# One fewer second-level token pair in two weight groups of a spectral mixer, with the work around the group change re-timed

## The chip, the cores and the metric

The kernel runs on one core of a Trainium2 chip. The metric is the device time of one execution in microseconds; the time of a kernel is the median of several executions. The engines named below are TensorE (PE, with its weight loads as PEld), VectorE (DVE), ScalarE (ACT), GpSimd (POOL) and SyncE (SP). SP and POOL issue the transfers.

## The reference

The kernel computes, for two batches of 4096 tokens of width 640, a gated mix of two branches:

```python
x = A_x
g = _sigmoid((x * gate_w).sum(-1, keepdims=True))
a = _A_ref(x, A_w1, A_b1, A_w2, A_b2)     # FFT over tokens, block-diagonal complex MLP, soft shrinkage, inverse FFT
b = _B_ref(x, B_w_gate, B_w_up, B_w_down) # (gelu(x @ w_gate) * (x @ w_up)) @ w_down, hidden width 1728
return g * a + (1 - g) * b
```

All arithmetic keeps about float32 precision. The kernel gets that from the matmul type fp32r by splitting each operand into a high and a low part and summing three products (high·high, high·low, low·high).

## The kernel before, in words

The first third of the span, and the place of the change, is the product `x @ [w_gate, w_up]` of branch B. The 8192 tokens are cut into 16 *token pairs* of 512 columns (two halves of 256). The hidden width is cut into 14 *weight tiles* of 128 columns, each with a gate and an up matrix, and the tiles are handled in three *groups*: tiles 0 to 3, 4 to 7 and 8 to 13. `keys` lists the (group, token pair) steps: steps 0 to 15 are group 0, steps 16 to 31 group 1 (token pairs in the order 1, 2, 0, 3, ... 15), steps 32 to 47 group 2. Each step calls `quad` once per weight tile (`plain` in step 0).

`quad` computes gate and up for both halves of a token pair with a Strassen-like scheme: seven block products in place of eight, on sums and differences ("forms") of token blocks (`b11`, `k4`, `t3`, `b21`, `t2`, `t5`, `t1`, `b22`, `t4`) and of weight blocks (`g1`, `g2`, `s1` to `s4`, `u2`). A call is 54 matmuls of 128x256. Part of its work (`half5`, `half3`, `half4`) is put off into the next call.

There is a second level. For the product of `g2` with `b21`, two token pairs (an odd one and the following even one) and two weight tiles form another 2x2 block, which `deep_parts` does with seven products instead of eight, 21 matmuls instead of 24. `deep(key)` says where: groups 0 and 1, token pairs 3 to 14. A deep `quad` leaves out its own six matmuls on `b21` and keeps partial results (`PB`, `h`) until the seven products have been added in (L695); these products are slipped into the next three calls by `extra`. Token forms for the second level are made by `x_deep` in group 0 (sums, then five split parts), stored to `xA` in memory, and loaded again in group 1; weight forms are made by `w_deep`.

The order of work is written out by hand. Each `quad` has seven hooks, so a step of groups 0 and 1 has 28 *slots*. `spread(i, s, fs)` puts functions into slots of step `i` from slot `s` on, running over into the next step; `at(i, j, f)` runs one after call `j` of step `i`. Each engine takes its instructions in the order in which they are written. What is placed so:

- `x_prep(nxt, k)` makes form `k` of the next step's token pair: a source (a VectorE subtraction or a raw tile), a high part on ScalarE, a low part on VectorE. In group 0 the forms `t1` to `t4` are also stored to `xD` through POOL's queue, and in most of group 1 they are loaded from there on SP's queue.
- `x_raw` loads the raw token tiles of the step after next, at the end of a step.
- `w_raw(t)` loads the two raw matrices of a weight tile of the next group; `w_prep(t)` makes its forms in eight stages.
- The forward Fourier transform of branch A is spread over steps 17 to 45 as 64 *elements* (`a_seq`), each a load `a_load`, two splits `a_split`, a gate sum `a_gate` and two halves of products `a_step`. `steps_a` says in which step an element sits, `A_POINTS` in which slots. Its tables come in four loads `f1_load`, the first three of which belong to elements 0, 18 and 38 and the last to 58.

On-chip buffers are pools of equal slots: 18 "big" (weights, `PB`, Fourier tables), 14 "mid" (token forms), 18 "small" (raw tiles, sums, `h`, Fourier data), 15 "tiny". A new tile waits until the last user of its slot is done. Stores are collected by `st` and issued on SP's queue at the end of the next call.

After these 48 steps follow the spectral MLP (L983 to L1124), and the down projection fused with the inverse transform (L1406, L297); the change does not touch their code.

Of the kernel before, what the change touches and what calls it, by code (L numbers as in the profile page):

```python
# [10 lines left out]
F32 = mybir.dt.float32  # L11
# [4 lines left out]
P = 128  # L16
# [7 lines left out]
CW = CH + 2  # L24
NCH = 8
NPAIR = 13
FIRST = 3

# [184 lines left out]
def spectral_mix_kernel(ctx: ExitStack, tc: tile.TileContext, a):  # L215
# [9 lines left out]
    dram = ctx.enter_context(tc.tile_pool(name="dram", bufs=1, space=bass.MemoryType.DRAM))  # L225
# [29 lines left out]
    def flush():  # L255
        for dst, src in late:
            ld(dst, src)
        late.clear()
# [5 lines left out]
    hD = dram.tile([64, P, 14 * P], F32, name="hD")  # L264
    wdf = [dram.tile([P, 13 * 320], F32, name=f"wdf_{j}") for j in range(7)]
    wdl = dram.tile([P, 7 * 320], F32, name="wdl")
    xA = {t: dram.tile([P, 3584], F32, name=f"xA_{t}") for t in range(FIRST, 15, 2)}

    fny = consts.tile([P, 8], F32, name="fny")
    sgn = consts.tile([P, 4], F32, name="sgn")  # L270
# [36 lines left out]
    GR, WA, XA, PEND = {}, {}, {}, {}  # L307

    def deep(key):
        return key[0] < 2 and FIRST <= key[1] < 15  # L310

    def w_raw(t):
        RAW[t] = []
# [132 lines left out]
    def x_raw(key, names=("b11", "b21", "b12", "b22", "k4")):  # L446
        d = XT.setdefault(key, {})
        for n in names:
            if (key[0] != 1 or made(key) or n != "b12") and not (key[0] == 1 and deep(key) and n == "b21"):
                r = d[n] = small([P, 512], name="xraw")  # L450
                ld(r, a["xT"][key[1], ("b11", "b21", "b12", "b22", "k4").index(n)])
# [6 lines left out]
    def x_prep(key, k, eng=nc.vector):  # L458
# [35 lines left out]
        def lo():  # L494
# [4 lines left out]
            if kept is not None:  # L499
                nc.gpsimd.dma_start(xD[key[1]][:, kept],  # L500
                                    XM.pop((key, name)).rearrange("p h n -> p (h n)").bitcast(F32))
        return [lambda: None] * 3 if name == "b21" and deep(key) else [src, hi, lo]

    def x_deep(gr, tp):
# [77 lines left out]
    def quad(key, t, hook):  # L582
# [7 lines left out]
        old = Q.pop() if Q else [lambda: None] * 3  # L590

        dp = deep(key)
        ahead_ = dp and key[1] % 2 == 1
        X = half()
# [167 lines left out]
    def mixed(key):  # L762

        o, w = XO[key], WG[NPAIR]
        ws = [(w[:, k, 0], w[:, k, 1]) for k in range(5)]
        pm = bank()
        for q, (x0, x1) in enumerate((("b11", "b21"), ("b12", "b22"))):
            run(pm[:, 256 * q:256 * q + 256], prod(ws, x_of(o, x0, x1, ("k4", q))))
        s, h = small([P, 512], name="gelu"), small([P, 512], name="h")
        nc.gpsimd.memset(h[64:], 0.0)  # L770
        nc.scalar.activation(s[:64], pm[:64], AF.Gelu_apprx_tanh)
        nc.scalar.activation(h[:64], pm[64:], AF.Copy)
        nc.vector.tensor_mul(h[:64], s[:64], h[:64])
        h_store(key[1], NPAIR, h)
# [713 lines left out]
    def at(i, j, f, *args):  # L1488
        todo.setdefault((i, j), []).append((f, *args))
# [57 lines left out]
    def spread(i, s, fs):  # L1547

        for k, f in enumerate(fs):
            j, q = i, max(s + k, 0)  # L1550
            while j < last and q >= points(j):
                j, q = j + 1, q - points(j)
            slots.setdefault((j, q), []).append(f)
    steps_a = [(i, j) for i in (*range(17, 30), *range(32, 46)) for j in ((0, 1) if i < 32 else (0, 1, 2) if 32 < i < 43 else (0, 2))]

    def back(i, s, f):
        if s < 0:
# [2 lines left out]
    for k, (b, n2) in enumerate(a_seq):  # L1560
        i, j = steps_a[k]
# [16 lines left out]
    for i, (gr, tp) in enumerate(keys):  # L1578
        if deep((gr, tp)) and tp % 2:
            p, f = x_deep(gr, tp)  # L1580
# [9 lines left out]
    for k, (l, pb) in enumerate(((1, 0), (1, 1), (2, 0), (2, 1))):  # L1590
        s0 = (5, 12, 19, 26)[k]
        f = prep(l, pb)
# [2 lines left out]
        spread(last, s0 + 1, f[2:])  # L1595
    for gr in range(2):
        for k, t in enumerate(groups[gr + 1]):
            (i, j), (i2, s) = [((14, 1), (15, 0)), ((14, 3), (15, 8)), ((15, 0), (15, 17)), ((15, 2), (16, 4)), ((15, 3), (16, 12)), ((15, 1), (15, 25))][k]
            at(16 * gr + i, j, w_raw, t)
            spread(16 * gr + i2, s, w_prep(t))  # L1600
    for j in range(7):
# [6 lines left out]
    for i, key in enumerate(keys):  # L1608
        gr, tp = key
        nxt = keys[i + 1] if i < last else None  # L1610
        quads = [t for t in groups[gr] if t < NPAIR]
        nq = len(quads)
        if nxt:
            if not i:
                x_raw(nxt)
            z = 7 * (nq - 1)
            for k, s in enumerate((5, 8, 11, 14, 16, 18, z + 1, z + 4, z + 6) if gr < 2 else
                                  (6, 9, 13, 17, 21, z + 1, z + 2, z + 3, z + 3, z + 5)):
                if k < 9 or nxt[0] == 2:
                    f0, f1, f2_ = x_prep(nxt, k)  # L1620
                    spread(i, s - 1, [f0])
                    spread(i, s + 1, [f1, f2_])
            if gr < 2 and nxt[0] == 2:
                spread(i, z + 7, x_prep(nxt, 9))
        for j, t in enumerate(quads):
            def hook(k):
                for f in slots.get((i, 7 * j + k), ()):
                    f()
            (quad if i else plain)(key, t, hook)
            if gr == 2 and j == 1:  # L1630
                mixed(key)
            if i % 16 == 15:
                WG.pop(t)
            if 0 < i + 1 < last and j == nq - 1:
                x_raw(keys[i + 2])
            n = len(late)
            for f, *args in todo.get((i, j), []):
                f(*args)
            new = late[n:]
            del late[n:]  # L1640
            flush()
            late.extend(new)
        for q in range(7 * nq, 7 * nq + 14) if i == last else ():
            for f in slots.get((i, q), ()):
                f()
        XO.pop(key)
# [131 lines left out]
```

## Time and profile before

| what | value |
|---|---|
| median of three runs | 2539.72 us (2539.08 to 2541.27) |
| the profiled execution | 2539.19 us, its span 2537.4 us |
| TensorE clock granted | 1.00 throughout |
| matmuls on PE | 20227, busy 2526.0 us |
| VectorE / ScalarE / POOL busy | 2085.4 / 1491.6 / 388.7 us |
| DMA | 502.65 MB, mean 198 GB/s |

Step 15, the last of group 0, lies at about 370 to 400 us from the start of the span; step 31, the last of group 1, at about 781 to 811 us.

In the profile, L562 is a product inside `quad`, L694 one of the second level, L817 one of the Fourier transform. L278 and L281 are the helpers that write the high and the low part of a split, so their lines are told apart by the tile: `xo` token forms, `xs` either a second-level token form or Fourier data, `w` weight forms, with `wt` their sums and `wraw` the raw weights. L588 and L589 copy or apply gelu to a result; L616, L640, L650, L651, L655 and L659 are VectorE's additions and multiplications on results. A row of the timeline ends in the idle time before the instruction and what ended it.

### The profile page before, as it was taken

The page shows a single profiled execution, that of the slowest core. Times are in us where ns is not written, and L with a number is a line of the kernel's source. Part 1 is how long each engine was busy: PE and PEld are TensorE (multiplying, and loading weights), DVE is VectorE, ACT ScalarE, POOL GpSimd, SP SyncE. Part 2 cuts the span into 40 slices and gives each one's busy share as a digit, 9 for nine tenths or more (in the row PEclk, how much of TensorE's full clock was granted, in tenths as well). Part 3 has the DMA queues.
Part 4 walks back from the last instruction along what each step waited for, and adds up shares of the span by engine and source line. Part 5 has one row for each costly group of instructions (what it writes and reads, how often), then busy time and mean ns, then how long its engine had stood idle before and what let it go on. Part 6 is the DMA issues. An engine that isn't in the chain of part 4 may idle for free.

```text
span 2537.4 us, 54692 instructions
## 1 busy us (share of the span) xinstructions
PE 2526.0 (100%) x20227; PEld 2517.4 (99%) x20227; DVE 2085.4 (82%) x4340; ACT 1491.6 (59%) x3504; POOL 388.7 (15%) x409
## 2 busy tenths in 40 slices
PE   9999999999999999999999999999999999999999
PEld 9999999999999999999999999999999999999999
DVE  7677778777777877787667788888999999999998
ACT  5455556656555666666556788777654444444443
POOL 0111110000000000000003111111133333333332
PEclk9999999999999999999999999999999999999999
DMA  6566667777777677777767454548744444344433
GB/s 217 206 209 232 229 226 217 241 236 240 232 253 249 208 236 247 242 236 226 230 220 228 123 167 139 167 144 267 275 152 151 156 155 142 132 151 156 155 126 104
DMA packets 352511, 502.65 MB, mean 198 GB/s; under 512 B 26284, under 2 KB 223532, under 8 KB 352244
## 3 DMA queue, kind: packets, MB, share of 16 engines
q1 hardware_dynamic: 334244, 446.33, 54.5%
q0 software_dynamic: 18000, 52.83, 5.7%
q8 instruction: 159, 2.61, 0.4%
q14 instruction: 108, 0.88, 0.1%
HBM read 308.41 MB, written 190.65 MB: 197 GB/s over the span
## 4 chain that ended last, share of the span: by engine, by line
PE 93%; DVE 3%; DMA 2%; ACT 1%; issue 1%; SPq 0%; DVEq 0%; ACTq 0%
PE bank L562 49%; PE bank L1406 22%; PE bank L297 14%; PE bank L983 3%; PE bank L694 2%; PE bank L817 1%; PE bank L1064 1%; PE bank L1065 1%; DVE w L281 1%; DMA xraw<-in_xT_dram 0%; DMA s<-scr 0%; DMA xo<-xD 0%; DVE xo L281 0%; DMA hD<-h 0%; PE bank L1066 0%
## 5 line engine op out<-in xcount | busy, mean ns | idle before, releaser
L562 PE MATMUL bank<-xo,w 128*128 128x256 f32 x11100 | 1316.5, 277 | 3.7 <-ACT u L588 1.6
L562 PEld LDWEIGHTS bank<-xo,w 128*128 128x128 f32 x11100 | 1291.6, 188 | 6.6 <-ACT u L588 2.8
L1406 PE MATMUL bank<-wx,ho 128*128 128x320 f32 x3844 | 560.7, 306 | 0.0
L1406 PEld LDWEIGHTS bank<-wx,ho 128*128 128x128 f32 x3844 | 557.1, 188 | 0.0
L281 DVE TENSOR_TENSOR ho<-hraw,ho 128x640 fp32r<-128x640 f32 (+3 forms) x384 | 266.4, 735 | 20.9 <-ACT ho L278 17.9
L278 ACT ACTIVATE ho<-hraw 128x640 fp32r<-128x640 f32 x320 | 167.0, 571 | 93.6 <-PE bank L1406 70.4
L588 ACT ACTIVATE u<-bank 128x256 f32<-128x256 f32 x312 | 119.7, 384 | 154.1 <-PE bank L562 144.3
L281 DVE TENSOR_TENSOR xs<-xr,xs 64x640 fp32r<-64x640 f32 x128 | 104.9, 820 | 73.1 <-ACT xs L278 71.1
L640 DVE TENSOR_TENSOR u<-bank,u 128x256 f32<-128x256 f32 x204 | 85.8, 421 | 85.6 <-ACT u L588 83.7
L281 DVE TENSOR_TENSOR xo<-xraw,xo 128x512 fp32r<-128x512 f32 x191 | 131.2, 687 | 22.3 <-ACT xo L278 21.0
L297 PE MATMUL bank<-wm,h 128*128 128x320 f32 (+1 forms) x792 | 137.9, 309 | 0.0
L819 DVE TENSOR_TENSOR as<-bank,as 64x320 f32<-64x320 f32 x256 | 113.7, 482 | 23.5 <-ACT as L818 21.7
L278 ACT ACTIVATE xo<-xraw 128x512 fp32r<-128x512 f32 x191 | 119.6, 626 | 14.8 <-DMA xraw<-in_xT_dram 10.5
L297 PEld LDWEIGHTS bank<-wm,h 128*128 128x128 f32 (+1 forms) x792 | 117.9, 185 | 1.5 <-DVE h L1042 0.3
L562 PE MATMUL bank<-wx,ho 128*128 128x320 f32 x764 | 116.7, 307 | 0.8 <-DVE ho L281 0.8
L562 PEld LDWEIGHTS bank<-wx,ho 128*128 128x128 f32 x764 | 112.1, 188 | 1.3 <-DVE ho L281 1.1
L818 ACT ACTIVATE as<-bank 64x320 f32<-64x320 f32 x256 | 96.8, 427 | 24.1 <-PE bank L817 20.4
L588 ACT ACTIVATE p<-bank 128x256 f32<-128x256 f32 x132 | 50.7, 384 | 95.6 <-DVE h L651 53.2
L278 ACT ACTIVATE xs<-xr 64x640 fp32r<-64x640 f32 x128 | 94.0, 735 | 21.3 <-DMA xr<-in_x_dram 19.2
L278 ACT ACTIVATE ho<-hs 128x640 fp32r<-128x640 f32 (+1 forms) x128 | 68.5, 569 | 63.6 <-DVE ho L281 44.9
L770 POOL MEMSET h<- 64x512 f32 x16 | 8.4, 522 | 615.9 <-PE bank L817 314.0
L1373 ACT ACTIVATE uu<-bank,gs 128x320 f32<-128x320 f32 x120 | 54.8, 526 | 75.1 <-PE bank L297 74.5
(196 smaller groups left out, 4008.0 us busy)
## 6 DMA issues: line engine op xcount, KB each, us to landing
xo<-xD SPq DMA_DIRECT2D x124, 512.0 KB
xraw<-in_xT_dram SPq DMA_DIRECT2D x213, 256.0 KB
hD<-h SPq DMA_DIRECT2D x176, 256.0 KB
hraw<-hD SPq DMA_DIRECT2D x128, 320.0 KB
xD<-xo POOLq DMA_DIRECT2D x64, 512.0 KB, 3.6
sc<-scr SPq DMA_DIRECT2D x65, 320.0 KB
xr<-in_x_dram SPq DMA_DIRECT2D x64, 320.0 KB
scr<-as SPq DMA_DIRECT2D x64, 320.0 KB
```

The costliest lines, as they stand in the source:

```text
L278: nc.scalar.activation(dst, src, AF.Copy, scale=scale)
L281: eng.tensor_sub(dst, src, hi.bitcast(F32))
L297: nc.tensor.matmul(dst, l, r, start=i == 0, stop=i == len(ops) - 1)
L562: nc.tensor.matmul(dst, l, r, start=first and i == 0, stop=i == len(ops) - 1, skip_group_check=True)
L588: copy = lambda d, s_: nc.scalar.activation(d, s_, AF.Copy)
L640: nc.vector.tensor_add(u4, C, u4)
L694: nc.tensor.matmul(acc, l, r, start=first and i == 0, stop=i == 2, skip_group_check=True)
L818: nc.scalar.activation(stg[hi, cs], pa[lo, :320], AF.Copy)
L819: nc.vector.tensor_add(stg[hi, cs], pa[hi, :320], stg[hi, cs])
L983: nc.tensor.matmul(pz[:, kp * P:(kp + 1) * P], SC[b, c, kp][:, o:o + P], ft, start=True, stop=True)
L1373: nc.scalar.activation(uu[n2][:, cs], pe[:, :320], AF.Copy, scale=gs[:, b, 0, n2:n2 + 1])
L1406: nc.tensor.matmul((X, Y)[k], *op, start=n[k] == 0 and not (more and k), stop=n[k] == tot[k] - 1, skip_group_check=True)
```

## The change

- `deep` now ends before token pair 13: pairs 13 and 14 of groups 0 and 1 do the product of `g2` and `b21` inside `quad`. So `x_deep` and the `xA` buffer exist for pairs starting at 3, 5, 7, 9 and 11 only, and `b21` is loaded and split for pairs 13 and 14 in group 1 too.
- The first weight tile of the next group (tile 4 in group 0, tile 8 in group 1) has its raw load at the end of step 13 (29) instead of after call 1 of step 14 (30), and its preparation in slots 10 to 17 of step 14 (30) instead of slots 0 to 7 of step 15 (31).
- The first Fourier element is placed in step 14; all others move up by one place, and step 42 has two places instead of three. The loads of the tables move with them.
- Where the step is deep and the next one is not (pair 12 to 13), the forms with number above 5 (`t1`, `b22`, `t4`) of the next pair come three slots later.

```diff
-FIRST = 3
+FIRST, LAST = 3, 13
...
-    xA = {t: dram.tile([P, 3584], F32, name=f"xA_{t}") for t in range(FIRST, 15, 2)}
+    xA = {t: dram.tile([P, 3584], F32, name=f"xA_{t}") for t in range(FIRST, LAST, 2)}
...
     def deep(key):
-        return key[0] < 2 and FIRST <= key[1] < 15
+        return key[0] < 2 and FIRST <= key[1] < LAST
...
-    steps_a = [(i, j) for i in (*range(17, 30), *range(32, 46)) for j in ((0, 1) if i < 32 else (0, 1, 2) if 32 < i < 43 else (0, 2))]
+    steps_a = [(i, j) for i in (14, *range(17, 30), *range(32, 46)) for j in ((0,) if i < 16 else (0, 1) if i < 32 else (0, 1, 2) if 32 < i < 42 else (0, 2))]
...
         for k, t in enumerate(groups[gr + 1]):
-            (i, j), (i2, s) = [((14, 1), (15, 0)), ((14, 3), (15, 8)), ((15, 0), (15, 17)), ((15, 2), (16, 4)), ((15, 3), (16, 12)), ((15, 1), (15, 25))][k]
+            (i, j), (i2, s) = [((13, 3), (14, 10)), ((14, 3), (15, 8)), ((15, 0), (15, 17)), ((15, 2), (16, 4)), ((15, 3), (16, 12)), ((15, 1), (15, 25))][k]
...
             for k, s in enumerate((5, 8, 11, 14, 16, 18, z + 1, z + 4, z + 6) if gr < 2 else
                                   (6, 9, 13, 17, 21, z + 1, z + 2, z + 3, z + 3, z + 5)):
+                if k > 5 and deep(key) and not deep(nxt):
+                    s += 3
```

## The prediction

> **What bounds the kernel now.** I read the page first: busy times, then the chain.
>
> ```profile
> span 2537.4 us, 54692 instructions
> PE 2526.0 (100%) x20227; PEld 2517.4 (99%) x20227; DVE 2085.4 (82%) x4340; ACT 1491.6 (59%) x3504; POOL 388.7 (15%) x409
> PE 93%; DVE 3%; DMA 2%; ACT 1%; issue 1%; SPq 0%; DVEq 0%; ACTq 0%
> ```
>
> TensorE sets the time nearly everywhere; the chain leaves it for 7%. So every matmul added is paid, and all that can be won lies in the places where TensorE was held up. To find them I asked for equal stretches and looked for low matmul counts. The columns are stretch, its length, busy time (instructions) of PE, PEld, DVE, ACT, POOL, then clock, DMA share, GB/s. First a stretch at full pace, then the five poor ones, with a good counterpart (703.20) to one of them (651.20).
>
> ```profile
> 300.00:325.00 25.00, 25.00 (x223) 25.00 (x223) 18.79 (x43) 12.78 (x33) 4.82 (x9) 1.00 0.74 261
> 344.00:370.00 26.00, 25.69 (x226) 25.49 (x225) 19.16 (x42) 14.39 (x36) 5.35 (x10) 1.00 0.74 263
> 370.00:400.40 30.40, 28.80 (x236) 27.50 (x235) 27.24 (x78) 18.25 (x54) 1.06 (x2) 1.00 0.73 218
> 651.20:674.30 23.10, 23.01 (x193) 22.31 (x193) 15.33 (x34) 12.78 (x30) 0.00 (x0) 1.00 0.87 317
> 703.20:725.05 21.85, 21.85 (x194) 21.85 (x193) 15.72 (x35) 13.10 (x30) 0.00 (x0) 1.00 0.83 300
> 753.80:769.40 15.60, 14.56 (x128) 14.36 (x127) 5.91 (x13) 6.08 (x15) 0.00 (x0) 1.00 0.96 326
> 781.50:811.40 29.90, 28.82 (x238) 27.44 (x237) 26.74 (x77) 17.84 (x54) 0.00 (x0) 1.00 0.80 255
> ```
>
> The pace of a matmul comes from PE's timeline: 152 of them from 339.83 to the next group at 357.06, 17.23/152 = 0.1134 us each.
>
> ```profile
> 339.83 17.39 PE L562 MATMUL bank<-xo,w 128*128 128x256 f32 x152
> 357.06 0.50 PE L694 MATMUL bank<-xo,w 128*128 128x256 f32 x3
> ```
>
> A plain call of `quad` is 54 matmuls, a call under the second level 48, and each 2x2 block has seven products of three. Step 15 (370.0 to 400.4, the last token pair of group 0) is 4x54 + 21 = 237 matmuls, 26.9 us; it took 30.4, so **3.5 us are lost**. Step 31 (781.5 to 811.4) is the same work: **3.0 us**. The stretch at 753.80 holds about 126 (14.3 us) in 15.6: **1.3**. The one at 651.20 does the work of the one at 703.20 in 1.25 us more. Step 14 adds 0.5 (five matmuls short).
>
> Now the causes. In step 15 VectorE first stands and then never stops (its timeline, PE's beside it, then three quads of the step in the columns above):
>
> ```profile
> 375.34 0.50 PE L694 MATMUL bank<-xs,w 128*128 128x256 f32 x3
> ...
> 372.37 0.42 DVE L346 TENSOR_TENSOR wt<-wraw 128x256 f32<-128x256 f32 x1
> 375.88 0.43 DVE L347 TENSOR_TENSOR wt<-wt,wraw 128x256 f32<-128x256 f32 x1 [3.09 <-PE bank L694]
> ...
> 378.70:386.60 7.90, 7.84 (x65) 7.47 (x65) 7.87 (x25) 5.22 (x16) 0.27 (x1) 1.00 0.87 251
> 386.60:393.80 7.20, 6.63 (x55) 6.32 (x54) 7.20 (x21) 4.83 (x15) 0.00 (x0) 1.00 0.53 137
> 393.80:400.40 6.60, 6.43 (x55) 6.22 (x55) 6.57 (x20) 4.46 (x16) 0.53 (x1) 1.00 0.86 268
> ...
> 787.45 0.43 DVE L347 TENSOR_TENSOR wt<-wt,wraw 128x256 f32<-128x256 f32 x1 [3.09 <-PE bank L694]
> ```
>
> L347 writes a new "small" buffer for the first weights of the next group. It waits 3.09 us for L694, a product of the second level that reads `xs`, a small buffer too: all 18 are taken. After it VectorE owes three preparations, and is at 7.87 of 7.90, 7.20 of 7.20, 6.57 of 6.60. Step 31 repeats this to the hundredth.
>
> **The change, part by part.** *Plain products for pairs 13 and 14, groups 0 and 1.* Eight `quad` calls per group gain 6 matmuls each and lose two blocks of 21: +6 per group, +12 in all, 12 x 0.1134 = **+1.4 us**, with no cover.
>
> On VectorE this takes the block additions (L695, 14 per group) and the low parts of `x_deep` out of steps 14 and 15, and gives each quad one addition (L616). The prices, from the list of groups by form, then one weight preparation's `wt` instructions, and a plain step with two Fourier elements:
>
> ```profile
> L819 DVE TENSOR_TENSOR as<-bank,as 64x320 f32<-64x320 f32 x256 | 113.7, 482 | 23.5 <-ACT as L818 21.7
> L281 DVE TENSOR_TENSOR xs<-xr,xs 64x640 fp32r<-64x640 f32 x128 | 104.9, 820 | 73.1 <-ACT xs L278 71.1
> L804 DVE SCALAR_TENSOR_TENSOR xr<-xr,gw 128x640 f32<-128x640 f32 x64 | 52.2, 816 | 0.3
> L281 DVE TENSOR_TENSOR xo<-xraw,xo 128x512 fp32r<-128x512 f32 x191 | 131.2, 687 | 22.3 <-ACT xo L278 21.0
> L695 DVE TENSOR_TENSOR pb<-bank,pb 128x256 f32<-128x256 f32 x120 | 50.3, 419 | 1.3 <-PE bank L694 1.1
> L616 DVE TENSOR_TENSOR p<-bank,p 128x256 f32<-128x256 f32 x108 | 46.7, 433 | 9.6 <-PE bank L562 7.2
> ...
> 384.80:393.30 8.50, 4.01 (x12) 1.00 0.52 146
> ...
> 448.50:473.00 24.50, 24.50 (x209) 24.50 (x208) 19.07 (x42) 14.74 (x35) 1.06 (x2) 1.00 0.72 225
> ```
>
> *First weights half a pair sooner.* `w_prep` of weight tile 4 (and 8) moves from slots 0-7 of step 15 (31) to slots 10-17 of step 14 (30). It costs VectorE 4.01 for `wt` and, as estimates from the 0.82 and 0.42 rows, 1.24 for the two low parts taken from `wraw`: 5.2 us, a little high because neighbours overlap. Step 15's VectorE then has 27.24 - 5.2 - 8 block additions x 0.42 = 18.7 us of work in 4x54x0.1134 = 24.5 us, and the 3.09 us wait has no `xs` left to wait for. In group 1, `b21` of 13 and 14 is now split in steps 28 and 29 (0.69 each), where the rows from 651.20 to 753.80 show VectorE a third idle: 0. What is late next in step 15 is the pair of preparations at slots 8-25, about as long as the 2.4 quads they share; I leave 0.3 us. Step 15: -3.5 + 0.3 = **-3.2**; step 31: -3.0 + 0.3 = **-2.7**. Bounds: all of it (-6.5) and nothing. I stay near the whole since both causes are removed, not shortened.
>
> *What step 14 now carries.* The first Fourier element moves from step 17 into step 14: two splits, one gate, four additions, 2x0.82 + 0.82 + 4x0.48 = 4.4 us. Its VectorE load: 19.16 + 5.2 + 4.4 + 4x0.43 - six block additions (2.5) - five `x_deep` low parts (two of 512 columns at 0.69, three of 256 at 0.42, 2.6) = 25.4 by durations, some 23 with the overlap of neighbours, in 25.1 us of TensorE work. The plain step at 448.50 with two elements loses nothing at 19.07. So it is tight: bounds 0 and 2.3 (the load by durations plus 2 us of idle as in that stretch), taken **+0.5**, nearer the row that lost nothing. Step 30 has no element and a light load: 0. The other elements each move up one place, and step 42 has one fewer: the same work, 0.
>
> *The forms made later.* In step 14 the copy for `t2` waits for the 15th "mid" buffer (there are 14) until the next quad's first product has read `b11`:
>
> ```profile
> 362.84 1.18 PE L562 MATMUL bank<-xo,w 128*128 128x256 f32 x9
> 364.67 2.33 PE L562 MATMUL bank<-xo,w 128*128 128x256 f32 x18 [0.31 <-ACT h L588]
> ...
> 363.71 0.63 ACT L278 ACTIVATE xo<-xd 128x512 fp32r<-128x512 f32 x1 [4.20 <-PE bank L562]
> ```
>
> That is the step from a deep pair to a plain one, worth the 0.5 us lost in step 14. It moves to step 12, and only `t1`, `b22`, `t4` come three slots later, which `t2` does not profit from: 0, bounds ±0.5. In group 1 the same wait stands on SP's queue (a load of `t2`), now in step 28, where stores of `hD`, `scr` and the next loads of `xr` and `xraw` queue behind it for some 4 us; they have a quad of lead: **+0.2**, bounds 0 and 1.3 (the loss at 753.80).
>
> *Transfers.* For pair 13 the five loads of `xA` go (2x512 + 3x256 = 1792 KB) and two of `b21` come (512 KB); as many stores leave POOL's queue.
>
> ```profile
> f<-in_f_dram POOLq DMA_DIRECT2D x3, 640.0 KB, 7.0
> xo<-xA SPq DMA_DIRECT2D x12, 512.0 KB
> xs<-xA SPq DMA_DIRECT2D x18, 256.0 KB
> ...
> 754.78 0.38 SPq L524 DMA_DIRECT2D xs<-xA  x1
> 757.72 2.25 SPq L451 DMA_DIRECT2D xraw<-in_xT_dram  x4
> 764.75 0.63 ACT L278 ACTIVATE xo<-xraw 128x512 fp32r<-128x512 f32 x1 [3.35 <-DMA hD<-h]
> 765.71 3.68 PE L562 MATMUL bank<-xo,w 128*128 128x256 f32 x30 [1.04 <-ACT p L588]
> ...
> 649.06 0.54 POOL L782 DMA_DIRECT2D f<-in_f_dram  x1 [191.43 <-DMA xr<-in_x_dram]
> 661.81 0.63 ACT L278 ACTIVATE xo<-xraw 128x512 fp32r<-128x512 f32 x1 [2.42 <-DMA xraw<-in_xT_dram]
> ```
>
> At 757.72 four `xraw` are issued behind the `xA` loads with the queues 96% busy; the first is used 7 us later, and TensorE stands 1.04. Without those 1.3 MB net the first tile should land in time: -1.3 + 0.1 = **-1.2**. The second Fourier table (`f`, 640 KB) was issued at 649.06 just ahead of the `xA` and `xraw` loads, and the wait at 661.81 follows; its good twin at 703.20 has no table load. It is now asked for 17 slots (15 us) earlier, at the start of step 25, and goes out once a "big" buffer is free: between 0 and -1.25, taken **-0.8**. The first table moves to step 13, where a big buffer is free: 0. The earlier raw weights (two of 320 KB) go where the `xA` traffic was: 0.
>
> Here the Trainium skill speaks against me. DMA: Bandwidth & Descriptors, section Anatomy of one DMA, fits a load from POOL as 2.0 us plus its bytes at 436 GB/s, an estimate of 3.5 us for this table, half of the measured 7.0. By that the table is no burden, the -0.8 falls away, and the sum would be 2534.7.
>
> **The sum**: 1.4 - 3.2 - 2.7 + 0.5 + 0.2 - 1.2 - 0.8 = -5.8 us. This execution took 2539.19 (span 2537.4 and 1.8 around it), which gives 2533.4; the median of the runs is 2539.72, 0.5 above, so I say **2533.9**.
>
> **Rivals.** *There is less to win.* PE's busy columns show idle of 1.60, 1.08, 1.04 and 0.09 in steps 15, 31, at 753.80 and at 651.20, 3.8 in all, where my counts say 9.05. If only that returns: 1.4 - 3.8 + 0.7 = -1.7, 2538.0. Against it: 237 matmuls at the pace seen elsewhere fit no other length. The Trainium skill, Perfetto Trace Analysis, section Identifying the Most-Contended Engine, calls matmul busy time a poor measure and load-weights busy time a good one; PEld idles 2.90, 2.46, 1.24 and 0.79, and by it the sum is 1.4 - 7.4 + 0.7 = -5.3, 2534.4, near mine.
>
> *VectorE only moves its jam.* Step 14 fills up by the 2.3 of its upper bound and step 15's pair of preparations keeps half of each loss: 1.4 - 3.25 + 2.3 + 0.2 - 2.0 = -1.4, 2538.3.
>
> *The change doesn't do what it says*: the small buffers are short at slot 10 too, and the 3 us wait comes along with both jams: 1.4 + 0.7 - 2.0 = +0.1, 2539.8. Against it: the three `xs`, and the `h` buffers that deep quads hold for three quads, are gone by then.
>
> *Slower.* The weights wait for big buffers. Of 18, twelve hold the old weights; the Fourier table now occupies one from step 13 on and the early preparation takes three more from slot 10. Should the preparations of steps 15 and 31 find none, ScalarE stands at each until a quad has released its weights, up to 5 us; the 4.20 us wait at 363.71 cost TensorE only 0.5, so some 2.4 us are covered and 2.6 lost. It decides from three preparations per group on: 6 x 2.6 = 15.6 in place of the 6.5 lost now, +15.6 - 6.5 + 1.4 - 2.0 + 0.7 = +9.2, 2548.9. Against it: 12 + 1 + 3 leaves two, since the four buffers of the second level are free by then.
>
> **How the numbers follow.** This kernel's runs spread by 2.2 us; 0.2% is 5.1 us, about what a measurement can tell, so faster begins below 2534.6. Forecast 0.60, between 2531.2 (gains whole, no new cost: -7.7 from the execution, rounded down) and 2535.5, some nine tenths of it under the bound; less to win or a moved jam 0.24; no effect 0.06; slower 0.10. That is faster 0.55, same 0.35, slower 0.10. The range runs from 2531.2 to 2540.4, and leaves out the slow rival and little else.
>
> **What the trace after should show.** L694 ends one pair earlier in each group; L347 waits for nothing near the end of steps 15 and 31, whose VectorE busy time falls to about 19 us, and both take near 24.6 us; no stall at 753-769; the 4.2 us ScalarE wait appears in step 12; step 14 has VectorE over 22 us. I am wrong if step 14 or 28 shows TensorE gaps of microseconds, if `w` copies wait for TensorE at slot 10, or if those two stretches keep their length.

## The result and the profile after

The changed kernel took 2531.82 us (median of 18 executions, 2530.49 to 2544.26), the kernel before in the same set 2540.49 (18 executions): a ratio of 0.9964, 95% interval 0.9947 to 0.9982. A second set gave 2533.60 against 2538.37, 0.9983 (0.9965 to 1.0001). The times of each kernel fall in two bunches some 11 us apart, for a reason given in the last section, and a median moves with the number that fall in each; "lower bunch" below means the median of the lower one alone. It is 2531.1 and 2531.3 for the changed kernel in the two sets, 2539.1 and 2538.1 for the kernel before: 7 to 8 us, 0.3%, are gained.

The profiled execution took 2531.49 us. The first rows of its page:

```profile
span 2529.7 us, 54653 instructions
PE 2522.0 (100%) x20239; PEld 2516.3 (99%) x20239; DVE 2078.9 (82%) x4323; ACT 1492.6 (59%) x3503; POOL 387.3 (15%) x404
PE 95%; DVE 2%; DMA 2%; ACT 1%; issue 0%; SPq 0%; DVEq 0%; ACTq 0%
```

There are twelve matmuls more, as counted, and PE's share of the chain rises from 93 to 95%. The stretches that were poor, in the columns used for the kernel before (steps 14 and 15, then steps 30 and 31):

```profile
349.40:374.30 24.90, 24.50 (x213) 24.16 (x212) 23.11 (x56) 16.62 (x41) 1.59 (x3) 1.00 0.59 206
374.30:398.80 24.50, 24.50 (x219) 24.50 (x218) 20.37 (x57) 15.62 (x42) 1.06 (x2) 1.00 0.85 272
756.20:780.70 24.50, 24.50 (x219) 24.50 (x218) 15.16 (x40) 12.56 (x35) 0.00 (x0) 1.00 0.66 219
780.70:805.20 24.50, 24.50 (x219) 24.50 (x218) 19.37 (x54) 15.35 (x42) 0.00 (x0) 1.00 0.84 280
```

PE's timeline of the same places, with the ScalarE copy that held it up in step 12 and the first wait-free `wt` of the new group:

```profile
316.75 2.33 PE L562 MATMUL bank<-xo,w 128*128 128x256 f32 x18 [0.31 <-ACT h L588]
357.83 11.18 PE L562 MATMUL bank<-xo,w 128*128 128x256 f32 x97
369.40 60.01 PE L562 MATMUL bank<-xo,w 128*128 128x256 f32 x525 [0.40 <-ACT u L588]
753.45 56.74 PE L562 MATMUL bank<-xo,w 128*128 128x256 f32 x499
...
315.80 0.63 ACT L278 ACTIVATE xo<-xd 128x512 fp32r<-128x512 f32 x1 [4.20 <-PE bank L562]
...
360.56 0.42 DVE L347 TENSOR_TENSOR wt<-wt,wraw 128x256 f32<-128x256 f32 x1
```

The 525 matmuls from 369.40 run through steps 15 and 16 without a wait that the timeline shows, and the 499 from 753.45 through the old stalls at 753 to 769 and 782 to 811. At the pace of 0.1134 us, 97 matmuls from 357.83 end at 368.83; the next starts at 369.40, so step 14 loses 0.57 us there. The 525 last 59.85 us, to the next product at 429.25, which is 0.3 above the pace; about 0.2 of it falls at 372, still in step 14. Where the two traces stand apart is read from the starts of the same instruction in both:

| instruction on PE | before | after | difference |
|---|---|---|---|
| first Fourier product of step 17 | 430.56 | 429.25 | -1.31 |
| a Fourier product of step 25 | 648.15 | 645.99 | -2.16 |
| the first second-level product behind it that both have, step 28 | 717.74 | 714.84 | -2.90 |
| first Fourier product of step 32 | 816.36 | 810.03 | -6.33 |
| first product of the spectral MLP (L983) | 1351.80 | 1345.54 | -6.26 |
| end of the span | 2537.4 | 2529.7 | -7.7 |

At -1.31 the changed kernel has already done one Fourier element more. The last 1.4 us come at the start of the down projection (1805 to 1825), whose code and data the change leaves alone.

### The profile page after: what moved, and what is told of

The parts are those of the page before. It is cut to its first block, busy times and chain, and to the rows that moved or that the text cites. A ratio compares the mean times of both kernels' runs of the same rounds, so it can differ in the third digit from the quotient of the medians.

```text
span 2529.7 us, 54653 instructions
## 1 busy us (share of the span) xinstructions
PE 2522.0 (100%) x20239; PEld 2516.3 (99%) x20239; DVE 2078.9 (82%) x4323; ACT 1492.6 (59%) x3503; POOL 387.3 (15%) x404
## 4 chain that ended last, share of the span: by engine, by line
PE 95%; DVE 2%; DMA 2%; ACT 1%; issue 0%; SPq 0%; DVEq 0%; ACTq 0%
PE bank L562 52%; PE bank L1406 22%; PE bank L297 14%; PE bank L983 3%; PE bank L694 2%; PE bank L817 1%; PE bank L1064 1%; PE bank L1065 1%; DMA xraw<-in_xT_dram 0%; DMA wdf<-wf 0%; PE bank L1066 0%; DMA scr<-as 0%; DMA zl<-zl 0%; DVE xo L281 0%; DMA wx<-wdf 0%
## 5 line engine op out<-in xcount | busy, mean ns | idle before, releaser
L281 DVE TENSOR_TENSOR ho<-hraw,ho 128x640 fp32r<-128x640 f32 (+3 forms) x384 | 260.8, 720 | 23.1 <-ACT ho L278 20.2
L588 ACT ACTIVATE u<-bank 128x256 f32<-128x256 f32 x328 | 125.5, 383 | 174.6 <-PE bank L562 166.4
L281 DVE TENSOR_TENSOR xs<-xr,xs 64x640 fp32r<-64x640 f32 x128 | 105.0, 820 | 75.8 <-ACT xs L278 73.6
L281 DVE TENSOR_TENSOR xo<-xraw,xo 128x512 fp32r<-128x512 f32 x194 | 133.2, 687 | 16.4 <-ACT xo L278 15.1
```

What stands on the lines that cost most here:

```text
L281: eng.tensor_sub(dst, src, hi.bitcast(F32))
L588: copy = lambda d, s_: nc.scalar.activation(d, s_, AF.Copy)
```

## The experiments

My theory was that of the prediction: steps 15 and 31 lose time because a `wt` waits for a small buffer while VectorE then owes three preparations beside the additions of the second level, and that plain products and early weights remove this together. The rivals: the plain products alone do it; the early weights cost what they bring.

### Plain products alone

```diff
-FIRST = 3
+FIRST, LAST = 3, 13
...
-    xA = {t: dram.tile([P, 3584], F32, name=f"xA_{t}") for t in range(FIRST, 15, 2)}
+    xA = {t: dram.tile([P, 3584], F32, name=f"xA_{t}") for t in range(FIRST, LAST, 2)}
...
-        return key[0] < 2 and FIRST <= key[1] < 15
+        return key[0] < 2 and FIRST <= key[1] < LAST
```

The Fourier places, the weights and the forms stay as they were in the kernel before.

> Only the plain products for pairs 13 and 14; weights, Fourier elements and forms stay where they were. My theory (the 3.09 us wait for a small buffer and the crowd of VectorE work in step 15 both cost): the wait of L347 is gone and VectorE loses 8 additions, but three weight preparations still meet in step 15, so steps 15 and 31 take about 25.7 us each (24.5 without loss) and the whole is 3 to 4.5 us faster than before. Rival, the preparations alone make the loss: steps 15 and 31 stay at 27 us or more and the whole moves by less than 2 us. Rival, the plain products are all that counts: 24.5 us per step and 6 us faster, as the full change. The stretch around the table load (step 25 to 26) keeps its loss of 1.25 us under all three.

Measured: 2532.25 us, ratio 0.9963 (0.9940 to 0.9987), lower bunch 2531.4 against 2538.5. PE's timeline through steps 14 to 17 and 29 to 31, the `wt` that had waited 3.09 us, and the window of step 15, in which the three weight preparations meet:

```profile
346.42 91.28 PE L562 MATMUL bank<-xo,w 128*128 128x256 f32 x804
763.03 56.74 PE L562 MATMUL bank<-xo,w 128*128 128x256 f32 x499
...
385.40 0.42 DVE L347 TENSOR_TENSOR wt<-wt,wraw 128x256 f32<-128x256 f32 x1
...
383.20:407.70 24.50, 24.50 (x218) 24.50 (x218) 23.85 (x68) 17.76 (x51) 1.06 (x2) 1.00 0.73 226
```

804 matmuls run without a hold-up, 0.1133 us each (91.12 us up to the Fourier product at 437.54). L347 waits for nothing, though it stands at its old place. VectorE is at 23.85 of 24.50 us while the three preparations meet, and TensorE loses nothing by it. So the early weights are not needed for this gain, and a full VectorE by itself does not hold TensorE up here: my expectation that about 1 us would be left in each of the two steps missed, and the rival (the plain products are all that counts) held.

### The change without its early weights

```diff
-            (i, j), (i2, s) = [((13, 3), (14, 10)), ((14, 3), (15, 8)), ((15, 0), (15, 17)), ((15, 2), (16, 4)), ((15, 3), (16, 12)), ((15, 1), (15, 25))][k]
+            (i, j), (i2, s) = [((14, 1), (15, 0)), ((14, 3), (15, 8)), ((15, 0), (15, 17)), ((15, 2), (16, 4)), ((15, 3), (16, 12)), ((15, 1), (15, 25))][k]
```

> The full change, but the first weight tile of the next group is loaded and prepared where it was before. My theory: steps 15 and 31 take about 25.7 us in place of the 24.5 of the full change, step 14 loses nothing (VectorE below 20 us there), so 2 to 2.5 us less is won than by the full change. Rival, the plain products are all that counts: the same time as the full change within 0.6 us. Rival, the preparations alone make the loss: steps 15 and 31 at 27 us or more, most of the gain gone (5 us).

> The change without its early weights, once more beside the change itself. If the early weights and nothing else cause the 0.57 us that TensorE loses at the end of step 14, step 14 is without loss and the time is 0.6 to 1.4 us under that of the change. If they are worth what I said in the prediction (part of 3.2 and 2.7 us), it is longer by 1 us or more.

Measured: 2530.45 and 2530.42 us, ratios 0.9965 (0.9943 to 0.9987) and 0.9962 (0.9943 to 0.9982); lower bunch 2529.7 and 2529.5. The changed kernel itself, repeated in the second set, had 2531.3 there:

> The changed kernel once more, to set it beside the two others of this set on the same chip: 2531 to 2532. If the down projection's first stall of the kernel before (0.84 us at L281) is a matter of the change, this trace is without it again, and the time from there to the end is 1.5 us shorter than before; if it varies from execution to execution, it may be back.

The first run's trace at the place where the changed kernel loses 0.57 us:

```profile
368.95 70.68 PE L562 MATMUL bank<-xo,w 128*128 128x256 f32 x622
```

These are the 97 matmuls and the 525 in one piece: the loss is gone, with the first Fourier element still in step 14. I had expected 2 to 2.5 us less gain; that missed. So the early weights win nothing and cost that loss. In the second set the two traces stand 0.9 us further apart after steps 14 to 16 than before them; of their whole distance of 2.5 us the rest lies where the kernels are the same, so I take 0.6 to 0.9 us as the price of the early weights, and not the 1.5 to 1.8 between the medians.

As for the end: the repeated trace of the changed kernel again lacks the 0.84 us at L281. That wait of the down projection stands in four of the fourteen traces of this study: 0.84 and 0.23 us in the two with pairs 13 and 14 on the second level (the second of them comes below), 0.47 and 0.29 in two of the twelve without. So it varies from execution to execution, and whether the change makes it rarer these runs can't tell.

### The Fourier elements and tables as before

```diff
-    steps_a = [(i, j) for i in (14, *range(17, 30), *range(32, 46)) for j in ((0,) if i < 16 else (0, 1) if i < 32 else (0, 1, 2) if 32 < i < 42 else (0, 2))]
+    steps_a = [(i, j) for i in (*range(17, 30), *range(32, 46)) for j in ((0, 1) if i < 32 else (0, 1, 2) if 32 < i < 43 else (0, 2))]
```

> The full change, but with every Fourier element, and so the table loads, in the steps where they were before. My theory: step 14 loses nothing (the 0.6 us lost at its end goes), the second table is again asked for in slot 17 of step 25 and the loss of about 1.2 us at step 26 returns, so the sum is 0.6 us slower than the full change and hardly to be told by the clock; the two stretches show it. Rival (the table is no burden for the other transfers): step 26 stays as in the full change and the whole is 0.6 us faster than it. Rival (the loss at the end of step 14 comes from the early weights alone): it stays.

Measured: 2535.20 us, ratio 0.9976 (0.9952 to 1.0001), lower bunch 2532.7. The same stretch of steps 25 and 26, from the start of a run of 61 matmuls to a Fourier product behind it, takes 23.07, 22.97 and 22.87 us in the kernel before, with plain products alone and here, all with the table where it was (the two variants of the kernel before and of the plain products that come below have 23.06 and 23.70). It takes 22.33 and 22.02 in the two traces of the changed kernel and 21.84 to 22.08 in seven of its variants, all with the table earlier. So the Fourier elements' places, the table's load among them, win 0.5 to 1.2 us in that stretch; the waits shown in the part on the transfers point to the load, but no run moves it alone. In step 14, now without the Fourier element but with the early weights, TensorE is still held up, for less, where I had expected nothing:

```profile
336.11 31.78 PE L562 MATMUL bank<-xo,w 128*128 128x256 f32 x279
368.05 59.99 PE L562 MATMUL bank<-xo,w 128*128 128x256 f32 x525 [0.15 <-ACT u L588]
```

279 matmuls from 336.11 end at 367.75 at the pace, so 0.30 us are lost there. That makes 0.57 us with both, 0.30 with the weights alone, nothing with the element alone: it takes both for the full loss.

### The forms not later

```diff
-                if k > 5 and deep(key) and not deep(nxt):
-                    s += 3
```

> The full change without the three slots by which t1, b22 and t4 of pair 13 come later. My theory: it was worth nothing, because the wait in step 12 is for the buffer of t2, which is not moved: the same 4 us wait of ScalarE, the same 0.5 us loss of TensorE, the same time within 0.5 us. Rival (the later forms hold off a second wait for mid buffers): another ScalarE wait of 2 to 4 us appears late in step 12, TensorE loses 1 us or more there, and in group 1 the SP queue stands again in step 28, 1 to 3 us slower in all.

Measured: 2531.69 us, ratio 0.9960 (0.9937 to 0.9982), lower bunch 2531.4. Both hold-ups of the changed kernel are there:

```profile
326.83 2.32 PE L562 MATMUL bank<-xo,w 128*128 128x256 f32 x18 [0.29 <-ACT h L588]
379.48 60.01 PE L562 MATMUL bank<-xo,w 128*128 128x256 f32 x525 [0.40 <-ACT u L588]
```

The later forms do nothing that can be seen.

### The jam taken apart: the wait without the additions

```diff
-            nc.vector.tensor_add(dst, acc, dst)
+            if tp < 13:
+                nc.vector.tensor_add(dst, acc, dst)
```

> The kernel before, with one thing left out: for the last pair of groups 0 and 1 VectorE does not add the seven products of the second level into the blocks (L695), 14 additions per group, 5.9 us of VectorE work. The output lacks these sums, so the time is that of a kernel that computes less. TensorE does the same matmuls, xs is read at the same place, and L347 still waits about 3.1 us for it. Theory A (the wait for the small buffer made the jam): steps 15 and 31 keep most of their loss of 3.5 and 3.0 us, at least 2 us each. Theory B (the wait alone is covered; it is the additions, which stand in the quads' way on VectorE, that hold TensorE up): both steps near 26.9 us, losses under 0.7. By B the span falls by some 5 to 6 us, by A by 1 to 2.

Measured: one execution of 2535.64 us. First PE in step 15 of the kernel before, then, in this run, VectorE's wait and PE:

```profile
373.30 0.50 PE L694 MATMUL bank<-xo,w 128*128 128x256 f32 x3
...
378.30 0.62 PE L694 MATMUL bank<-xo,w 128*128 128x256 f32 x3 [0.64 <-DVE pb L695]
...
392.47 6.41 PE L562 MATMUL bank<-xo,w 128*128 128x256 f32 x54 [0.57 <-ACT u L588]
...
430.56 0.45 PE L817 MATMUL bank<-xs,f 128*128 128x320 f32 x2
```

```profile
375.80 0.43 DVE L347 TENSOR_TENSOR wt<-wt,wraw 128x256 f32<-128x256 f32 x1 [3.76 <-PE bank L694]
...
373.22 0.50 PE L694 MATMUL bank<-xo,w 128*128 128x256 f32 x3
...
376.62 0.96 PE L562 MATMUL bank<-xo,w 128*128 128x256 f32 x6 [0.17 <-DVE u L640]
377.41 0.50 PE L694 MATMUL bank<-xo,w 128*128 128x256 f32 x3
...
390.41 29.76 PE L562 MATMUL bank<-xo,w 128*128 128x256 f32 x255 [0.25 <-ACT u L588]
...
428.51 0.45 PE L818 MATMUL bank<-xs,f 128*128 128x320 f32 x2
```

From 373.22 to 390.41 there are 141 matmuls, 16.0 us at 0.1134, in 17.2: 1.2 us lost, where the kernel before loses 3.2 over the same 141 (373.30 to 392.47). Counted on to the first Fourier product of step 17 (471 matmuls, 53.4 us), the loss is 1.9 us in place of 3.9, and in group 1, over the 249 matmuls up to the first one of step 32, 1.5 in place of 3.25. The wait is even longer than before (3.76 us) and VectorE as busy behind it, but the second-level products, which waited 0.64 us for L695 at 378.30, pass. Neither number of the expectation is met: about 2 us of each jam go with the additions and 1.5 to 1.9 stay, between the two theories.

### The jam taken apart: the wait put back without second-level products

```diff
+                if (i, 7 * j + k) in ((14, 13), (30, 13)):
+                    HELD.extend(small([P, 624], F32R, name="held") for q in range(6))
+                    for q in HELD:
+                        nc.gpsimd.memset(q.bitcast(F32), 0.0)
+                if (i, 7 * j + k) in ((15, 4), (31, 4)):
+                    hb = bank()
+                    for q in HELD:
+                        nc.tensor.matmul(hb[:, :256], q[:, :P], q[:, :256], start=True, stop=True)
+                    HELD.clear()
```

> The plain products alone (the kernel without the other parts of the change), with the shortage of small buffers put back: six of the 18 are taken at slot 13 of steps 14 and 30 and are read by one matmul each at slot 4 of steps 15 and 31, so that who asks for a small buffer in between waits. It adds six matmuls and six GpSimd fills per group, 0.7 us each group. Theory A (the wait made the jam): L347 waits 2 to 4 us at the start of steps 15 and 31 and both lose 2 to 3 us beyond the 0.7. Theory B (the wait is covered as long as the additions of the second level are not there): L347 may wait as long, but the steps lose under 0.7 us.

Measured: one execution of 2547.15 us (in the upper bunch). The wait is back in both groups, and PE behind it:

```profile
388.40 0.43 DVE L347 TENSOR_TENSOR wt<-wt,wraw 128x256 f32<-128x256 f32 x1 [2.72 <-PE bank L1634]
798.89 0.43 DVE L347 TENSOR_TENSOR wt<-wt,wraw 128x256 f32<-128x256 f32 x1 [2.73 <-PE bank L1634]
...
388.79 5.28 PE L562 MATMUL bank<-xo,w 128*128 128x256 f32 x45
394.83 25.45 PE L562 MATMUL bank<-xo,w 128*128 128x256 f32 x217 [0.77 <-ACT p L588]
...
799.28 5.28 PE L562 MATMUL bank<-xo,w 128*128 128x256 f32 x45
804.72 19.84 PE L562 MATMUL bank<-xo,w 128*128 128x256 f32 x171 [0.16 <-ACT p L588]
```

45 matmuls are 5.1 us; from 388.79 they take 6.04 and from 799.28 5.44: 0.9 and 0.3 us lost, not 2 to 3. A wait of 2.7 us on VectorE is mostly covered here, with nothing of the second level behind it on VectorE. So in group 0 the wait without second-level products costs 0.9, the wait with these products but without their additions 1.2, and the wait with both 3.2 over the same 141 matmuls: the loss of steps 15 and 31 was not the wait alone, and about half of it or more came with the additions. What the additions would cost without the wait, no run shows; so whether the two add up or make each other worse stays open. The plain products take both away at once. (Much of the rest of this run's longer time lies elsewhere: from 409 to 459 us it runs at the slower pace of the last section.)

### t2 and t5 later as well

```diff
+                if k in (4, 5) and deep(key) and not deep(nxt):
+                    s += 5
```

Added to the change without its early weights.

> The change with the first weights at their old place, and at the step from a deep pair to a plain one t2 and t5 made five slots later, so that t2's copy asks for the 15th mid buffer when b11 has been read. If the 0.3 to 0.5 us that TensorE loses in step 12 (in group 0) is that wait, it is gone: 0.3 to 0.5 us less there, and in group 1 up to 0.35 less in step 28, so about 2530 or a little under, by 0.5 to 0.9 less than with the weights late alone. If t2 then comes too late for the quad that reads it, TensorE waits for it instead and nothing is won or up to 1 us is lost.

> Late weights and t2 and t5 five slots later, beside the two others: no hold-up of TensorE from step 2 to step 16, where the others have 0.3 to 0.5 us in step 12; about 0.5 us under the late weights alone.

Measured: 2529.98 us twice, ratios 0.9954 (0.9935 to 0.9973) and 0.9979 (0.9961 to 0.9998); lower bunch 2530.0 and 2529.4. In both traces PE is held up nowhere from 52 to 430 us; the 0.31 us that waited for the mid buffer in step 12 is gone. Beside the version without it (2529.7 and 2529.5) the times show no difference, so the 0.5 us that I expected is not confirmed. The two versions with late weights are the fastest of the study; which of them is faster stays open.

### What wasn't tried

No run has the early weights with pairs 13 and 14 still on the second level, none the second table alone 17 slots earlier in the kernel before, and none the second-level additions without the wait for a small buffer. So what the early weights would do while the jam is there stays open.

## Why the prediction was right

The forecast, faster at 2533.9, held: the measured 2531.8 lies in the likeliest case's own range (2531.2 to 2535.5), near its edge of whole gains (which by its own terms, -7.7 from 2539.19, is 2531.5). The traces agree with its mechanism in steps 15 and 31, at 753 and at the table; the last 1.4 us, in the down projection, it did not foresee, and 0.84 of them is a wait that comes and goes between executions. That part is luck. By its steps:

| step of the sum | predicted | measured | from |
|---|---|---|---|
| 12 matmuls more | +1.4 | +1.4 | 20239 less 20227, at 0.1134 |
| step 15 | -3.2 | -3.5 | no hold-up left from 369.40 to 429 |
| step 31 | -2.7 | -3.0 | no hold-up left from 753.45 to 810 |
| step 14 | +0.5 | +0.9 | 0.57 from 368.83 to 369.40, 0.3 behind it |
| forms later; `t2`'s wait moves to step 12 | 0 | 0 | 0.47 lost at 316 for the 0.5 in step 14; experiment |
| change from deep to plain in group 1, step 28 | +0.2 | +0.5 | 714.84 to 727.86 after, 717.74 to 730.27 before; the repeat of the changed kernel has +0.1 |
| `xA` loads gone | -1.2 | -1.3 | no hold-up at 753 to 769 |
| second table earlier | -0.8 | -0.74 | -2.16 to -2.90 in the table above |
| sum | -5.8 | -5.7 | -6.26 at 1351.80 |
| down projection | 0 | -1.4 | 0.84 of it a wait that varies between executions |

The measured terms add up to within 0.6 us of the shift read at the spectral MLP, and no closer agreement is to be had from single traces: the kernel before ran a stretch of step 18 at a slower pace and lost 0.9 us that the execution after didn't lose, the execution after lost 0.7 us at 1150, and its repeat stands at -7.6 in place of -6.26 at the same product.

**The counts were the right measure of what there was to win.** The rival that took PE's busy columns (3.8 us, 2538.0) falls: 8.5 us of the 9.05 came back. The Trainium skill, Perfetto Trace Analysis, section Identifying the Most-Contended Engine, prefers the busy time of the weight loads to that of the matmuls; that was the better of the two here, with 7.4 us, and still short of the 8.5 that counting matmuls found.

**The step that failed is "First weights half a pair sooner".** It named both causes of the jam, the wait and the crowd on VectorE, but put their removal down to both edits and so left 0.3 us each in steps 15 and 31 for the two preparations that still meet. The plain products alone remove everything, with three preparations meeting at VectorE 23.85 of 24.50. The early weights contribute nothing and are, together with the Fourier element, what step 14 pays 0.57 us for. Without them the changed kernel is 0.6 to 0.9 us faster by the traces. My row for a covered load was the plain step at 19.07; the run with 23.85 and no loss shows that load on VectorE was not the quantity to look at. By the two runs that take the jam apart it is rather what waits for VectorE.

**The signs named for the trace** are there: no wait at L347, VectorE at 20.37 and 19.37 us where 19 were expected, both steps at the clean pace, VectorE at 23.11 in the stretch of step 14 that has the early weights.

**The mid buffer.** As said, the 4.20 us ScalarE wait went from step 14 to step 12 (315.80), and the three late forms changed nothing about it.

**The transfers.** The stall at 753 to 769 went with the `xA` loads. The table's load, in POOL's timeline after; this one load in the DMA issues of 620 to 660 us, first before, then after (KB each, us from issue to landing); and the wait for `xraw` after, which was 2.42 us before:

```profile
635.01 0.53 POOL L782 DMA_DIRECT2D f<-in_f_dram  x1 [178.84 <-DVE pb L695]
...
f<-in_f_dram POOLq DMA_DIRECT2D x1, 640.0 KB, 8.9
f<-in_f_dram POOLq DMA_DIRECT2D x1, 640.0 KB, 5.6
...
657.69 0.64 ACT L278 ACTIVATE xo<-xraw 128x512 fp32r<-128x512 f32 x1 [0.47 <-DMA xraw<-in_xT_dram]
```

It is issued 14 us sooner than at 649.06, 12 of them in the order of work; what let it go isn't settled, as this trace names L695 and the repeat a store of `hD`. With the table where it was, ScalarE waits 2.42, 2.07 and 1.91 us for `xraw` in the kernel before, with plain products alone and with the Fourier elements as before. The Trainium skill, DMA: Bandwidth & Descriptors, section Anatomy of one DMA, gives an estimate of 3.5 us for this load, by which the -0.8 would have fallen away. That did not hold here: the load takes 8.9 us before and 5.6 after, and every trace with the table moved is 0.5 to 1.2 us shorter in that stretch.

**The slow rival** needed a shortage of big buffers at slot 10. The copies of the new weights in step 14 go from 359.54 to 367 without a wait for TensorE, so it didn't arise. The jam that VectorE was to carry into step 14 by another rival came to 0.9 us of the 2.3 named there.

## What to carry to other kernels

Count matmuls against the clean pace to find what a stretch loses, and then ask for each waiting operation who stands behind it: here an engine at 97% cost nothing, a 2.7 us wait cost 0.9 or 0.3, and a 3.1 us wait together with additions that the next products needed cost 3.2. When a change bundles several edits, price each on its own: one edit here carried the gain, the Fourier elements' places with the table were worth 0.5 to 1.2 us, one nothing, and one took back 0.6 to 0.9.

## What was not expected: two paces of the matmul

In some executions the 128x256 matmuls of group 0 run 4% slower, at 117.7 ns in place of 113.4, with the granted clock at 1.00 (the third column from the right). One window of the change without its early weights, in its first traced execution:

```profile
100.00:125.00 25.00, 25.00 (x215) 25.00 (x214) 18.33 (x42) 12.55 (x31) 5.35 (x10) 1.00 0.63 232
```

The same window of the same kernel in its second:

```profile
100.00:125.00 25.00, 25.00 (x223) 25.00 (x222) 18.28 (x41) 13.55 (x33) 4.81 (x9) 1.00 0.71 257
```

215 matmuls in 25 us against 223, both without an idle moment. All four traced executions of the upper bunch run at the slower pace behind a hold-up of TensorE at 52 us, and none of the eight of the lower bunch does. In three of the four it ends at the next hold-up, at 326 us (step 12); 274 us at this pace are 10 us more, about the distance of the bunches. In the fourth, the slow trace above, that hold-up changes nothing, and the pace changes at 365, behind two Fourier products, where nothing waits:

```profile
326.80:351.80 25.00, 25.00 (x215) 25.00 (x214) 18.81 (x46) 12.58 (x33) 2.66 (x5) 1.00 0.57 180
...
347.04 18.54 PE L562 MATMUL bank<-xo,w 128*128 128x256 f32 x156
365.42 0.45 PE L817 MATMUL bank<-xs,f 128*128 128x320 f32 x2
365.70 3.12 PE L562 MATMUL bank<-xo,w 128*128 128x256 f32 x26
```

156 matmuls take 18.38 us up to the Fourier products, 117.8 ns each; the 26 behind take 2.96, 113.8 each. Two kernels tested whether a hold-up sets the pace, both with this edit at the start of some steps of the changed kernel:

```diff
+                    hz = tiny([P, 256], F32R, name="hold")
+                    nc.vector.memset(hz.bitcast(F32), 0.0)
+                    hb = bank()
+                    nc.tensor.matmul(hb[:, :256], hz[:, :P], hz, start=True, stop=True)
```

> The kernel after, with one more matmul at the start of steps 3, 5, 7 and 9 on a tile that VectorE has just cleared, which holds TensorE up for some tenths of a us each time (about +0.2 to +0.5 us each, 1 to 2 us in all). Theory P (TensorE comes out of a hold-up at one of two paces, 113.4 or 117.7 ns per 256-column matmul, and keeps it until the next hold-up): the pace may change at each of the four places, so one trace shows it constant between them and changing only there, and the times are no longer in two bunches 11 us apart but lie between, at steps of about 2 us (50 us of two steps at 4%). Theory Q (the pace of group 0 is set once per execution and a hold-up does not touch it): two bunches as before, 11 us apart, each 1 to 2 us up.

> The kernel after, with a matmul on a tile just cleared by VectorE at the start of each of the steps 2 to 11: ten hold-ups of 1.0 to 1.4 us. Theory P (a hold-up lets the pace of the matmuls change, and it stays until the next): the trace shows the stretches between them at 113.4 ns or at 117.7 ns a matmul, both kinds in one trace, and the changes only at the hold-ups. Theory Q (the pace of group 0 is set once per execution): all ten stretches at the same pace.

With four hold-ups the 12 times lie between 2535.72 and 2540.36, ratio 0.9976 (0.9959 to 0.9993): no bunch 11 us above, and a lowest time raised by the 5.1 us that the four cost (1.04 and three times 1.36; I had expected 1 to 2). With ten, one execution of 2546.67 us; its trace shows both paces and where they change. PE's timeline, with the inserted matmul at L1633:

```profile
160.69 0.38 PE L1633 MATMUL bank<-hold 128*128 128x256 f32 x1 [0.72 <-DVE hold L1631]
160.91 11.47 PE L562 MATMUL bank<-xo,w 128*128 128x256 f32 x96
...
179.63 2.28 PE L562 MATMUL bank<-xo,w 128*128 128x256 f32 x18
...
187.80 0.39 PE L1633 MATMUL bank<-hold 128*128 128x256 f32 x1 [1.29 <-DVE hold L1631]
...
194.84 2.20 PE L562 MATMUL bank<-xo,w 128*128 128x256 f32 x18
...
212.73 0.38 PE L1633 MATMUL bank<-hold 128*128 128x256 f32 x1 [0.72 <-DVE hold L1631]
212.95 11.05 PE L562 MATMUL bank<-xo,w 128*128 128x256 f32 x96
...
263.90 0.39 PE L1633 MATMUL bank<-hold 128*128 128x256 f32 x1 [0.72 <-DVE hold L1631]
264.12 11.47 PE L562 MATMUL bank<-xo,w 128*128 128x256 f32 x96
...
282.85 2.28 PE L562 MATMUL bank<-xo,w 128*128 128x256 f32 x18
```

18 matmuls take 2.28 us behind the first of these hold-ups, 2.20 behind the second and the third, and 2.28 again behind the one at 263.90; 96 take 11.47, 11.05 and 11.47. Within a stretch the pace stays. So in these stretches, which hold no Fourier products, TensorE comes out of a hold-up at one of two paces and keeps it until the next; the rows at 365 show that products of another shape can change it too. The length of a hold-up may count: all six hold-ups of 1.0 to 1.4 us in this trace are followed by the faster pace, three of the four of 0.72 us by the slower. Ten of them don't settle it, and the times with four long hold-ups still spread by 4.6 us. What decides, and what the two paces are, stays open; the granted clock is 1.00 in both.
